# Weights 96 instead of 64 bytes beyond the moving rows, modulo 128, in three stages of a float32r kernel

## The chip, the cores and the metric

The kernel runs on one core of a Trainium2 chip. Its time is the device time of one execution in microseconds; three runs of the kernel before gave 1219.47, 1219.58 and 1220.62 us, median 1219.58.

## The reference

Three layers follow one another; batch 4, sequence 448, width 768 (12 heads of 64).

```python
attn = 1 / (1 + np.exp(-(scale * q @ k.T - np.log(S))))   # sigmoid, per head
x = attn @ v                                              # heads side by side: (4, 448, 768)
xk, xr = (mu * x + (1 - mu) * x_prev for mu in (mu_k, mu_r))
x = 1 / (1 + np.exp(-(xr @ w_r))) * (np.maximum(xk @ w_k, 0) ** 2 @ w_v)
u = x + np.real(np.fft.fft(np.fft.fft(x, axis=1), axis=2))
un = (u - mean) / np.sqrt(var + 1e-06)
out = u + np.maximum(un @ w_ch1, 0) @ w_ch2               # w_ch1: 768 x 3072
```

All is float32. The kernel reaches that precision with float32r matmuls: each operand is split into a high and a low part, and a product is the sum of three matmuls, high by high, high by low and low by high.

## The kernel before, in words

`tile` (L183) makes one output tile of 128 rows by 448 tokens. For each part of the contraction it issues three matmuls: weights high with rows high, weights high with rows low, weights low with rows high. "Weights" are the stationary 128x128 block, "moving rows" the 448 tokens that stream past it. Each matmul has a weight load of its own, which runs while the matmul before it streams.

The stages, in order of time, with their PE tile names:

- attention (`sc`, `av`), with the keys stage (`k<-xkh,wkh` and so on) filled in between;
- receptance (`r<-xrh,wrh`): four batches of 6 x 6 x 3 = 108 matmuls, one after another, with the same weights;
- values (`v<-k,wvh`), with the Fourier stage of each batch in its gaps (`pa`, `qa`, `pq`, `sp`);
- the feed-forward network: first layer (`f<-un,w1h`, and for two of the batches seven products of sums, `f_X`, `f_Y`, `f_Z`, `f_W` `<-B,blk` or `<-T,blk`), second layer (`f<-h,w2h`, `f<-h,v2h`).

The class `Order` (L93) keeps a model of the engines' times and decides by it in which order instructions are issued. It knows sizes, not addresses.

Tiles come from pools that are stacked from the left or the right end of SBUF. A tile's address within its partition follows from what was taken before it in its pool and from the pools below it. `shift` (L256) takes a tile that nobody uses, 16 float32 or 64 bytes, as the first of a pool; all that comes after it in this pool, and in the pools that are stacked on it, lies 64 bytes further. Seven pools have such a tile: `mop` (L341, rows of the keys), `wvp` (L605, weights of the values), `norm` (L662), `wpa` (L964, weights of the second layer), `hp` (L966, hidden rows), `wpb1` (L968) and `wpb2` (L1274, weights of both layers).

Below, the **relation** of a matmul is the address of the weights that are loaded while it streams, less the address of its own moving rows, modulo 256. In the kernel before, by the addresses that the build gives to the tiles:

| stage | weights less rows, mod 128 | of these at relation 192 | at relation 64 |
|---|---|---|---|
| keys | 64 | 557 | 0 |
| receptance | 64 | 215 (batches 1 and 3) | 216 (batches 0 and 2) |
| values | 64 | 1 | 526 |
| network, first layer, `un` | 64 | 843 | 7 |
| network, first layer, `blk` | 64 | 425 | 331 |
| network, second layer, `w2` | 64 | 425 | 437 |
| network, second layer, `v2` | 64 | 425 | 433 |

(Counted are matmuls whose successor on PE is of these stages too; the 128-row score matmuls of the attention have relation 0 to each other and to the key weights that follow them, and the one step from receptance to values has relation 160.)

Of the kernel before, what the change touches and what calls it, by code (L numbers as in the profile page):

```python
# [12 lines left out]
F32 = mybir.dt.float32  # L13
# [231 lines left out]
def build(tc, ap):  # L245
# [5 lines left out]
    def pool(stack, name, bufs=1, side="left", space=None):  # L251
        if space is not None:
            return stack.enter_context(tc.tile_pool(name=name, bufs=bufs, space=space))
        return stack.enter_context(tc.tile_pool(name=name, bufs=bufs, side=side, reuse_waits="tile"))

    def shift(pl, name):  # L256
        pl.tile([128, 16], F32, tag="shift", name=f"shift_{name}", bufs=1)

    def load_split(pl, parts, gap=0.0, raws=1, lane=0, eng=None, vector=False, every=0.0):

# [77 lines left out]
    wra = pool(s_w, "wra", 1, "right")  # L338
    wkp = pool(s_l, "wkp", 1, "left")
    mop = pool(s_l, "mop", 2, "left")  # L340
    shift(mop, "mop")  # L341
    att = pool(s_r, "att", 2, "right")
    ps2 = pool(s_ps, "ps2", 5, space=PSUM)

# [257 lines left out]
    s_l, s_k = ExitStack(), ExitStack()  # L602
    kp = pool(s_k, "kp", 1, "left")
    wvp = pool(s_l, "wvp", 1, "left")
    shift(wvp, "wvp")  # L605
    wvh = wvp.tile([128, NF, D], F32R, name="wvh")
    wvl = wvp.tile([128, NF, D], F32R, name="wvl")

# [50 lines left out]

    s_r, s_f = ExitStack(), ExitStack()  # L660
    np_ = pool(s_r, "norm", 1, "right")
    shift(np_, "norm")  # L662
    wq = pool(s_r, "wq", 1, "right")
    fp = pool(s_f, "four", 1, "right")
    cd = fp.tile([128, 2, CW], F32R, name="cd")
# [295 lines left out]

    s_l = ExitStack()
    wpa = pool(s_l, "wpa", 2, "left")
    shift(wpa, "wpa")  # L964
    hp = pool(s_l, "hp", 2, "left")
    shift(hp, "hp")  # L966
    wpb1 = pool(s_l, "wpb1", 2, "left")
    shift(wpb1, "wpb1")  # L968
    acc, h_t = {}, {}

    def load_acc(b, *keys):
# [299 lines left out]
    s_f.close()  # L1271
    s_b, s_w = ExitStack(), ExitStack()
    wpb2 = pool(s_b, "wpb2", 2, "right")
    shift(wpb2, "wpb2")  # L1274
    tp = pool(s_b, "tp", 1, "right")
    wst = pool(s_w, "wst", 1, "right")
    pools_of = {"w1": (wq, wpb1), "w2": (wpa, wpb2)}
# [78 lines left out]
```

## Time and profile before

| | us |
|---|---|
| median of three runs | 1219.58 |
| the profiled execution | 1218.67 |
| its span, first to last instruction | 1216.9 |
| PE busy | 1203.2 (99%) |
| PE weight loads busy | 1048.5 (86%) |
| DVE busy | 906.9 (75%) |
| ACT busy | 479.3 (39%) |

A matmul's busy time on PE includes the time in its pipeline, so neighbours overlap. What a matmul costs in a dense stream is the distance between two starts, which is read below from stretches with a known number of matmuls. [...]

### The profile page before, as it was taken

The numbers are of one execution on the slowest core, as the hardware profiler recorded it, in microseconds if no ns is written. First come the engines' busy times: TensorE is split into PE (matmuls) and PEld (weight loads), VectorE is DVE, ScalarE is ACT, GpSimd is POOL, SyncE is SP. The second block draws the span as 40 slices with busy tenths as digits, with TensorE's granted clock in tenths as the row PEclk, the third lists the DMA queues.
The fourth block names the chain that finished last, engine by engine and source line by source line (L and its number), as shares of the span: only waits on it lengthen the run. The fifth ranks groups of instructions, "written<-read, shape, count | busy, mean of one in ns | idle before, by whom it ended". The sixth has DMA issues, their size and how long they took to land. (4 is left out here: it accounts for less than half of the span.)

```text
span 1216.9 us, 16416 instructions
## 1 busy us (share of the span) xinstructions
PE 1203.2 (99%) x6142; PEld 1048.5 (86%) x6142; DVE 906.9 (75%) x1425; ACT 479.3 (39%) x864; POOL 135.9 (11%) x97
## 2 busy tenths in 40 slices
PE   8999999999999999999989999999999999999998
PEld 3467767789999999999979999999999999999998
DVE  5676887656852569797999999998566776776654
ACT  5867767657640122142233233333132332322320
POOL 0000000000000000000223232322021111211110
PEclk9999999999999999999999999999999999999999
DMA  6657669666947546387555655655832112122102
GB/s 217 216 175 240 203 244 342 239 242 238 319 164 249 192 167 213 104 315 240 191 186 206 220 186 194 216 202 191 327 134 79 53 59 72 53 67 64 53 1 91
DMA packets 77296, 217.82 MB, mean 179 GB/s; under 512 B 9312, under 2 KB 31776, under 8 KB 76576
## 3 DMA queue, kind: packets, MB, share of 16 engines
q1 hardware_dynamic: 76544, 214.37, 50.9%
q0 software_dynamic: 672, 2.40, 0.6%
q8 instruction: 48, 0.79, 0.3%
q14 instruction: 32, 0.26, 0.1%
HBM read 143.84 MB, written 72.90 MB: 178 GB/s over the span
## 5 line engine op out<-in xcount | busy, mean ns | idle before, releaser
L215 DVE TENSOR_TENSOR acc<-acc,f 128x448 f32<-128x448 f32 x258 | 156.8, 617 | 60.3 <-PE f L180 57.1
L180 PE MATMUL f<-h,w2h 128*128 128x448 f32 x576 | 163.6, 365 | 4.2 <-DVE acc L215 4.2
L180 PE MATMUL f<-un,w1h 128*128 128x448 f32 x576 | 163.7, 364 | 0.0
L180 PE MATMUL f<-h,v2h 128*128 128x448 f32 x576 | 163.1, 364 | 0.0
L180 PEld LDWEIGHTS f<-h,w2h 128*128 128x128 f32 x576 | 107.5, 188 | 13.8 <-DVE acc L215 6.2
L234 ACT ACTIVATE sg<-sc,bias_s 128x448 f32<-128x448 f32 x168 | 95.2, 653 | 61.1 <-PE sc L180 61.1
L180 PEld LDWEIGHTS f<-h,v2h 128*128 128x128 f32 x576 | 108.1, 188 | 7.3
L180 PEld LDWEIGHTS f<-un,w1h 128*128 128x128 f32 x576 | 108.1, 188 | 7.3 <-issue 0.4
L180 PE MATMUL v<-k,wvh 128*128 128x448 f32 x384 | 112.9, 368 | 0.3 <-DMA k<-k_d 0.3
L180 PE MATMUL f<-h,w2l 128*128 128x448 f32 x288 | 104.5, 363 | 0.3 <-POOL w2l L215 0.3
L180 PE MATMUL f<-h,v2l 128*128 128x448 f32 x288 | 104.1, 362 | 0.0
L180 PE MATMUL f<-un,w1l 128*128 128x448 f32 x288 | 103.9, 361 | 0.0
L223 DVE SCALAR_TENSOR_TENSOR w_bits<-w_raw,w_bits 128x768 uint32<-128x768 uint32 x80 | 100.0, 1250 | 1.0
L180 PE MATMUL av<-sg,v 128*64 128x448 f32 (+1 forms) x336 | 81.1, 549 | 0.0
L180 PEld LDWEIGHTS v<-k,wvh 128*128 128x128 f32 x384 | 71.7, 188 | 6.8 <-DMA k<-k_d 1.1
L215 POOL TENSOR_TENSOR v2l<-v,v2h 128x768 fp32r<-128x768 f32 x24 | 47.0, 1975 | 271.7 <-ACT v2h L232 271.7
L215 POOL TENSOR_TENSOR w1l<-w,w1h 128x768 fp32r<-128x768 f32 x20 | 41.9, 2093 | 298.0 <-ACT w1h L232 298.0
L180 PE MATMUL v<-k,wvl 128*128 128x448 f32 x192 | 70.4, 367 | 0.0
L180 PE MATMUL k<-xkh,wkh 128*128 128x448 f32 x192 | 69.9, 364 | 0.0
L180 PE MATMUL k<-xkl,wkh 128*128 128x448 f32 x192 | 69.7, 363 | 0.0
L180 PE MATMUL k<-xkh,wkl 128*128 128x448 f32 x192 | 69.5, 362 | 0.0
L180 PEld LDWEIGHTS av<-sg,v 128*64 128x64 f32 (+1 forms) x336 | 27.8, 143 | 42.5 <-issue 36.0
(175 smaller groups left out, 2354.6 us busy)
## 6 DMA issues: line engine op xcount, KB each, us to landing
w_raw<-in_w SPq DMA_DIRECT2D x40, 768.0 KB, 4.8
w_d<-w SPq DMA_DIRECT2D x40, 384.0 KB, 2.5
k_d<-kp SPq DMA_DIRECT2D x32, 448.0 KB, 2.8
k<-k_d SPq DMA_DIRECT2D x32, 448.0 KB, 5.9
a<-w_d SPq DMA_DIRECT2D x24, 384.0 KB, 3.5
v<-w_d SPq DMA_DIRECT2D x24, 384.0 KB, 3.1
k<-in_k SPq DMA_DIRECT2D x24, 256.0 KB, 5.2
v<-in_v SPq DMA_DIRECT2D x24, 256.0 KB, 3.0
```

The costliest lines, as they stand in the source:

```text
L180: self.nc.tensor.matmul(out, lhs, rhs, start=start, stop=stop, skip_group_check=skip)
L215: eng.tensor_tensor(out, a, c, op=op)
L223: self.nc.vector.scalar_tensor_tensor(out, a, scalar, c, op0=op0, op1=op1)
L234: self.nc.scalar.activation(out, a, fn, **kw)
```

## The change

`shift` gets the number of float32 as an argument. The pools of moving rows get 8 (32 bytes), those of weights 24 (96 bytes); `norm` gets 8, since the tiles of the first layer's weights, `wq`, are stacked on it.

```diff
-    def shift(pl, name):
-        pl.tile([128, 16], F32, tag="shift", name=f"shift_{name}", bufs=1)
+    def shift(pl, name, n):
+        pl.tile([128, n], F32, tag="shift", name=f"shift_{name}", bufs=1)
-    shift(mop, "mop")
+    shift(mop, "mop", 8)
-    shift(wvp, "wvp")
+    shift(wvp, "wvp", 24)
-    shift(np_, "norm")
+    shift(np_, "norm", 8)
-    shift(wpa, "wpa")
+    shift(wpa, "wpa", 24)
-    shift(hp, "hp")
+    shift(hp, "hp", 8)
-    shift(wpb1, "wpb1")
+    shift(wpb1, "wpb1", 24)
-    shift(wpb2, "wpb2")
+    shift(wpb2, "wpb2", 24)
```

No instruction is added, removed or moved: the order on PE, DVE, ACT, POOL and SP is the same row for row. What changes are addresses. By the build's addresses, in keys, values and network the weights now lie 96 bytes beyond the rows modulo 128; modulo 256, all 2676 matmuls of relation 192 get relation 224, and all 1734 of relation 64 get relation 96. Receptance keeps its relations of 64 and 192, the scores theirs of 0. In the Fourier stage rows and weights move together by 32 bytes, and their differences stay.

## Rows read from the trace of the kernel before

**Rows 1.** The page's first part: busy time, share and instructions of each engine.
```profile
PE 1203.2 (99%) x6142; PEld 1048.5 (86%) x6142; DVE 906.9 (75%) x1425; ACT 479.3 (39%) x864; POOL 135.9 (11%) x97
```

**Rows 2.** Busy time of each engine by stage; columns in the first row.
```profile
core 0: us, PE busy (x) PEld busy (x) DVE busy (x) ACT busy (x) POOL busy (x), PEclk, DMA share, GB/s
0.00:330.00 330.00, 324.88 (x1618) 231.22 (x1619) 233.21 (x334) 230.29 (x436) 4.26 (x28) 1.00 0.70 241
...
400.00:590.00 190.00, 189.66 (x1104) 176.93 (x1103) 149.91 (x327) 49.77 (x98) 3.71 (x2) 1.00 0.57 197
590.00:760.00 170.00, 165.53 (x819) 152.73 (x818) 167.45 (x204) 57.74 (x87) 50.19 (x24) 1.00 0.58 203
760.00:1216.90 456.90, 453.12 (x2260) 422.46 (x2258) 323.80 (x510) 124.45 (x218) 74.81 (x38) 1.00 0.32 110
```

**Rows 3.** Timeline of PE and its loads in receptance: start us, us, engine, line, instruction.
```profile
302.90 0.37 PE L180 MATMUL r<-xrh,wrh 128*128 128x448 f32 x1
302.90 0.19 PEld L180 LDWEIGHTS r<-xrl,wrh 128*128 128x128 f32 x1
...
303.11 0.36 PE L180 MATMUL r<-xrl,wrh 128*128 128x448 f32 x1
303.11 0.19 PEld L180 LDWEIGHTS r<-xrh,wrl 128*128 128x128 f32 x1
```

**Rows 4.** Receptance batches 0, 1, 2 and 3, each of 108 matmuls; columns as in rows 2.
```profile
281.05:302.90 21.85, 21.85 (x109) 20.25 (x108) 12.94 (x21) 13.17 (x24) 0.00 (x0) 1.00 0.73 253
302.90:324.51 21.61, 21.61 (x109) 20.25 (x108) 18.60 (x27) 13.14 (x22) 0.00 (x0) 1.00 0.86 286
324.51:346.35 21.84, 21.84 (x110) 20.25 (x108) 16.25 (x24) 13.54 (x23) 0.00 (x0) 1.00 0.89 314
346.35:367.96 21.61, 21.61 (x109) 20.25 (x108) 8.68 (x11) 6.31 (x10) 0.00 (x0) 1.00 0.35 121
```

**Rows 5.** Groups of PE instructions, receptance batch 0: count | busy us, mean ns.
```profile
L180 PE MATMUL r<-xrl,wrh 128*128 128x448 f32 x36 | 13.2, 367 | 0.0
L180 PE MATMUL r<-xrh,wrh 128*128 128x448 f32 x36 | 13.1, 363 | 0.0
L180 PE MATMUL r<-xrh,wrl 128*128 128x448 f32 x36 | 13.0, 361 | 0.0
```

**Rows 6.** The same of receptance batch 3.
```profile
L180 PE MATMUL r<-xrh,wrl 128*128 128x448 f32 x37 | 13.3, 360 | 0.0
L180 PE MATMUL r<-xrl,wrh 128*128 128x448 f32 x36 | 13.1, 363 | 0.0
L180 PE MATMUL r<-xrh,wrh 128*128 128x448 f32 x36 | 13.1, 362 | 0.0
```

**Rows 7.** Timeline, network, first layer: 72 matmuls from one start to the other.
```profile
849.65 0.57 PE L180 MATMUL f<-un,w1h 128*128 128x448 f32 x2
...
864.05 0.57 PE L180 MATMUL f<-h,w2h 128*128 128x448 f32 x2
```

**Rows 8.** Timeline, network, second layer: 72 matmuls from one start to the other.
```profile
1198.19 0.36 PE L180 MATMUL f<-h,v2l 128*128 128x448 f32 x1
...
1212.75 0.37 PE L180 MATMUL f<-h,v2l 128*128 128x448 f32 x1
```

**Rows 9.** Groups by shape, whole span: third product of the scores and of the keys.
```profile
L180 PE MATMUL k<-xkh,wkl 128*128 128x448 f32 x192 | 69.5, 362 | 0.0
...
L180 PE MATMUL sc<-qh,kl 128*128 128x448 f32 x18 | 6.6, 368 | 0.0
```

**Rows 10.** Groups of the first values stretch, with receptance's last matmul.
```profile
L180 PE MATMUL r<-xrh,wrl 128*128 128x448 f32 x1 | 0.4, 370 | 0.0
```

## The prediction, made before the changed kernel ran

> **What bounds the kernel.** I read the busy times first: PE is busy for 99% of the span, and no other engine comes near it over the whole [rows 1]. The stretches by stage say where that could be otherwise [rows 2]. PE lacks 5.1 us of 330 in attention and keys, 0.3 of 190 in values and Fourier, 3.7 of 457 late in the network. Only between 590 and 760 us is another engine as full: DVE is busy for 167.45 of 170 us, PE for 165.53. So outside that stretch whatever PE's matmuls lose or gain goes into the end almost whole. The granted clock is 1.00 in all of these rows.
>
> Since nothing is reordered, the question is only what one matmul costs at another relation of addresses. The timeline shows why a relation could matter [rows 3]: the load of the next weights starts in the same 10 ns as the stream of the current rows, at 302.90 and at 303.11, and lasts 0.19 us of the 0.20 us to the next start. Both read the same memory at the same time.
>
> Receptance measures the relation in the kernel before. Its four batches have the same instructions, shapes, weights and number, 108 matmuls; batches 0 and 2 have relation 64 and batches 1 and 3 relation 192. They take 21.85, 21.61, 21.84 and 21.61 us [rows 4]. Divided by 108 that is 202.3 and 202.2 ns against 200.1 and 200.1. DVE busy (12.9, 18.6, 16.3, 8.7 us), ACT and the share of DMA do not follow this alternation, so traffic of other engines is not the cause. The groups of batches 0 and 3 show it in one matmul's length too: one of the three products has a mean of 367 ns at relation 64, none exceeds 363 at 192 [rows 5, 6]. The network repeats it: 72 matmuls of the first layer, relation 192, take 864.05 - 849.65 = 14.40 us or 200.0 ns each [rows 7]; 72 of the second layer at relation 64 take 14.56 us or 202.2 ns [rows 8].
>
> [...]
>
> **The change part by part.** Nothing is removed or added; shifts of 32 bytes move the matmuls to other relations: 2676 from 192 to 224 and 1734 from 64 to 96. DVE, ACT and DMA also work on tiles that lie 32 bytes elsewhere; I cost that at nothing, since they run beside PE, and only DVE between 590 and 760 us could show it, where it has 2.5 us to spare.
>
> Neither 96 nor 224 stands in the trace in a sustained stretch. The neighbours do.
>
> - For 224: on one side 192 at 200.1 ns, on the other 0 (that is 256). Relation 0 stands in the last product of the 128-row scores, ahead of a key matmul: mean 368 ns against 362 for the keys' third product at relation 192 [rows 9]. Pitch and length go together: in receptance batch 3 the mean length is (360 + 363 + 362) / 3 = 361.7 at a pitch of 200.1, so the length is the pitch plus 161.6, and 368 is a pitch of 206.4.
> - For 96: on one side 64 at 202.2, on the other 160, seen once: receptance's last matmul before the values, 370 ns [rows 10], a pitch of about 208.4.
>
> The rows at 0 and 160 are single places in a sequence, and at relation 64 one product in three reads 367 while the mean of all is 363.7; an average at 0 or 160 may thus lie some 3 ns below what is read. That puts 0 at about 203.4 and 160 at about 205.4. By a straight line, 224 is half the way from 192 to 256: 200.1 + 1.65 = 201.75. Without the correction it would be 203.25. 96 is a third of the way from 64 to 160: 202.2 + 1.05 = 203.25, without the correction 204.3.
>
> I take 1.9 ns more for relation 224, nearer to the corrected value since most matmuls hang on it, and 1.2 ns more for relation 96. The sum: 2676 x 1.9 = 5.1 us, and 1734 x 1.2 = 2.1 us, together 7.2 us. Of the 4410 matmuls about 800 lie in the stretch where DVE is as full as PE [rows 2]; their share of 7.2 us is 1.3, and PE's idle 4.5 us there can hide a part, of which I take 0.5. So the span grows by 6.7 us. The profiled execution took 1218.67 us, 1.8 us outside its span of 1216.9, and that remains; it is 0.9 us below the median of 1219.58. Against the median: 1219.58 + 6.7 = 1226.3 us, say 1226.
>
> Bounds of one matmul, from rows: below, the shortest product group of any stretch is 360 ns [rows 6], a pitch of 198.4; all 4410 there would be 2676 x 1.7 + 1734 x 3.8 = 11.1 us less, 1208.4. Above, all at 206.4 would be 2676 x 6.3 + 1734 x 4.2 = 24.1 us more, 1243.7. A gain can't be excluded: the relation that is best in the trace is known to be better than one other in sustained stretches only.
>
> **The rivals.**
>
> Only the half counts: the pitch depends on whether the weights are ahead by less or more than 128 bytes modulo 256, and anywhere in the lower half it is 202.2, in the upper half 200.1. For it speaks that keys and receptance, whose rows start at 32 bytes modulo 64, and the network, whose rows start at 0, have the same 200.0 to 200.1 at relation 192. Against it, that 0 reads high. Nothing would change: 1219.6 us. [...]
>
> Further ahead is better: the load's reads come clear of the rows sooner, and relation 96 falls to the 200.1 of 192 while 224 stays there. Place: the 1734 matmuls of the values, of half the second layer and of part of the first. Price: 1734 x 2.1 = 3.6 us less, of which some 0.3 is lost between 590 and 760 us, where DVE holds the chain; 1216.3 us. For it: 64 is the worst sustained relation that is known, so any step away from it may help. It decides as soon as relation 224 costs under 3.3 / 2676 = 1.2 ns more. If both fall below 200.1, to the 198.4 of the bound, the time is 1208.
>
> Both are as bad as relation 0: the places that read 368 and 370 are then the rule and 192 is a narrow good spot: 1243.7 us.
>
> **How the numbers follow.** Slower by the straight line, 1226: 0.42. No change, 1219.6: 0.19. Faster at 1216: 0.24, faster towards 1208: 0.07. Slower towards 1244: 0.08. From these, faster by over 0.2% has 0.31, within 0.2% 0.19, slower by over 0.2% 0.50; 0.2%, some 2.4 us, is about what a measurement of this kernel can tell from no change. The range of 8 in 10 leaves out about half of each far case and the edges of the others: 1211 to 1241. The likeliest case alone runs from 1222, where the steps are half as large, to 1231, where no correction is made for single places (2676 x 3.15 + 1734 x 2.1 = 12.1 us).
>
> **What would show it.** Receptance must keep 21.85 and 21.61 us a batch, since its relations stay; if it moves, addresses are not the whole of it. Keys, now all at 224, should show a pitch near 202 before receptance begins. The values, all at 96, should stand near 203.4. Stretches of 72 in the network should alternate between these two, no longer between 200.0 and 202.2. Weight loads should still start with the streams, and their own length stay at 0.19 us. I am wrong if either stretch of 72 comes out at or below its value before, and most of all if the two differ with opposite signs, for then relations would have to be measured one by one.

## The result and the profile after

The changed kernel takes 1231.4 us, median of five runs (1230.32 to 1231.85); the kernel before 1219.58 (1219.44 to 1220.62). The ratio is 1.0093, with a 95% interval of 1.0082 to 1.0105: slower by 11.8 us, where the forecast of 1226 us was 6.4 (and its sum 6.7). The profiled execution took 1231.40 us, 12.7 more than that of before.

The first part of the page, and below it the stages, to be read against [rows 1, 2]; the windows follow the stages, which end later now.

```profile
PE 1217.2 (99%) x6142; PEld 1049.7 (85%) x6142; DVE 907.9 (74%) x1425; ACT 479.1 (39%) x864; POOL 134.9 (11%) x97
```

```profile
0.00:332.00 332.00, 327.10 (x1617) 231.36 (x1618) 233.04 (x334) 230.19 (x436) 4.25 (x28) 1.00 0.70 239
...
402.00:592.00 190.00, 189.31 (x1099) 176.04 (x1098) 149.30 (x326) 49.23 (x96) 3.69 (x2) 1.00 0.57 197
592.00:764.00 172.00, 168.91 (x823) 154.05 (x822) 169.03 (x207) 58.98 (x88) 49.17 (x25) 1.00 0.57 201
764.00:1229.60 465.60, 461.85 (x2260) 422.82 (x2258) 323.76 (x508) 123.39 (x217) 74.85 (x38) 1.00 0.31 108
```

PE is busy for 14.0 us more; no other engine gained more than 1 us, and the loads of weights 1.2. So the matmuls themselves stand further apart. Where, the timeline says. The four batches of receptance, whose relations were kept, in windows as in [rows 4]:

```profile
283.16:305.00 21.84, 21.84 (x109) 20.25 (x108) 13.38 (x22) 13.12 (x24) 0.00 (x0) 1.00 0.75 255
305.00:326.60 21.60, 21.60 (x109) 20.25 (x108) 18.04 (x26) 13.02 (x22) 0.00 (x0) 1.00 0.87 285
326.60:348.45 21.85, 21.85 (x109) 20.25 (x108) 16.27 (x24) 13.49 (x23) 0.00 (x0) 1.00 0.89 315
348.45:370.06 21.61, 21.61 (x109) 20.25 (x108) 8.68 (x11) 6.29 (x10) 0.00 (x0) 1.00 0.35 119
```

They are as before to 0.01 us. Below are the starts at the ends of four dense stretches, from the timeline: 152 keys at relation 224, 162 matmuls of the values at 96, 72 of the first layer at 224, and 72 of the second at 96 [rows 7, 8 are the last two before].

```profile
252.76 0.36 PE L180 MATMUL k<-xkl,wkh 128*128 128x448 f32 x1
...
283.16 0.37 PE L180 MATMUL r<-xrh,wrh 128*128 128x448 f32 x1
...
370.06 0.37 PE L180 MATMUL v<-k,wvh 128*128 128x448 f32 x1
...
402.48 0.44 PE L180 MATMUL v<-k,wvh 128*128 128x448 f32 x1
...
855.62 0.36 PE L180 MATMUL f<-un,w1h 128*128 128x448 f32 x1
...
870.49 0.37 PE L180 MATMUL f<-h,w2h 128*128 128x448 f32 x1
...
1210.62 0.37 PE L180 MATMUL f<-h,v2l 128*128 128x448 f32 x1
...
1225.49 0.36 PE L180 MATMUL f<-h,v2l 128*128 128x448 f32 x1
```

That is 30.40 / 152 = 200.0 ns, 32.42 / 162 = 200.1, 14.87 / 72 = 206.5 and 14.87 / 72 = 206.5. The same relation has two prices: 224 costs 200.0 in these keys and 206.5 in the first layer, 96 costs 200.1 in the values and 206.5 at the end of the second layer. A matmul's mean length shows it too; first the stretch of the first layer at 206.5, then the keys at 200.0:

```profile
L180 PE MATMUL f<-un,w1h 128*128 128x448 f32 x46 | 13.4, 369 | 0.0
L180 PE MATMUL f<-un,w1l 128*128 128x448 f32 x23 | 8.5, 369 | 0.0
```

```profile
L180 PE MATMUL k<-xkh,wkh 128*128 128x448 f32 x46 | 16.7, 362 | 0.0
L180 PE MATMUL k<-xkh,wkl 128*128 128x448 f32 x46 | 16.7, 362 | 0.0
L180 PE MATMUL k<-xkl,wkh 128*128 128x448 f32 x45 | 16.3, 362 | 0.0
```

(These keys are the last of their stage, whose mean is 203.4.) Averaged over all neighbours in the traces that stand under 215 ns apart, relation 224 costs 205.35 ns (2664 of them) where 192 cost 200.19, and relation 96 costs 202.32 (1707) where 64 cost 202.16. That gives 13.7 + 0.3 = 14.0 us. PE's waits give some back: in the second layer (`w2`) what stands above a dense pitch fell from 6.2 to 3.9 us, in the values it rose from 2.7 to 3.4. 14.0 - 2.3 + 0.7 = 12.4 of the 12.7 us.

Two theories went into the experiments. Theory 1: each relation has one price. Theory 2, suggested by these stretches: at some relations a dense stretch of matmuls can settle at either of two pitches, 200.0 or 206.7 ns; it stays at the one it has, and what ran just before selects it.

### The profile page after: what moved, and what is told of

It is laid out like the page before. It is cut to its first block, busy times and chain, and to the rows that moved or that the text cites. A ratio compares the mean times of both kernels' runs of the same rounds, so it can differ in the third digit from the quotient of the medians.

```text
span 1229.6 us, 16416 instructions
## 1 busy us (share of the span) xinstructions
PE 1217.2 (99%) x6142; PEld 1049.7 (85%) x6142; DVE 907.9 (74%) x1425; ACT 479.1 (39%) x864; POOL 134.9 (11%) x97
## 5 line engine op out<-in xcount | busy, mean ns | idle before, releaser
L180 PE MATMUL f<-un,w1h 128*128 128x448 f32 x576 | 166.8, 370 | 0.0
```

The lines of the kernel that those rows point to most:

```text
L180: self.nc.tensor.matmul(out, lhs, rhs, start=start, stop=stop, skip_group_check=skip)
```

## The experiments

**Sixteen relations by themselves.** The stretch as it is written, abridged at `...`; `d` is the relation, `r0` is 0 here, and all addresses are in float32:

```python
r = [r0, r0 + S]
o = (d // 4 + r0) % 64
for t in range(n):
    j = t % KD
    w = [o + 128 * j, o + D + 128 * j]
    ...
    for i, (a, c) in enumerate(((0, 0), (0, 1), (1, 0))):
        nc.tensor.matmul(out, wts[:, w[a] : w[a] + 128], rows[:, r[c] : r[c] + S], ...)
```

> Leaves out the whole computation: it runs only float32r matmuls of the feed-forward network's form (128x128 weights, 448 rows moving, three products each), with no other engine at work, at sixteen relations of weights to moving rows (0 to 240 bytes in steps of 16, modulo 256), 72 matmuls a stretch, once upward, once downward, and then at eight relations each behind a stretch at 192, behind one at 0, and behind a rest of PE. Theory 1, the relation alone sets the price: every visit to a relation shows the same mean pitch, 202.2 ns at 64, 200.1 at 192, about 202.3 at 96 and 205.4 at 224, the means that the two kernels show. Theory 2, two states kept by history: at 96 and 224 a stretch runs either at 200.0 or at 206.7 ns throughout, and which one depends on what ran before it, so that visits to the same relation differ by 6.7 ns.

The pitch into which each stretch settles (mean of its last 30 starts), in ns; where two stand, visits differed:

| relation | 0 | 16 | 32 | 48 | 64 | 80 | 96 | 112 |
|---|---|---|---|---|---|---|---|---|
| ns | 202.7 or 206.7 | 206.7 | 204.4 | 202.2 | 202.2 | 203.3 | 200.0 or 206.7 | 204.0 |

| relation | 128 | 144 | 160 | 176 | 192 | 208 | 224 | 240 |
|---|---|---|---|---|---|---|---|---|
| ns | 204.0 | 204.4 or 202.2 | 205.3 | 203.3 | 200.0 | 204.4 | 200.0 or 206.7 | 203.3 |

The 64 and 192 of this kernel, with no other engine at work (202.2 and 200.0 ns), are those of the full kernel (202.16 and 200.19), so it takes no other engine to make the difference. Four relations have two prices. All values of the table are 200.0 ns plus a simple fraction of 6.67: 1/3 (202.2), 2/5 (202.7), 1/2 (203.3), 3/5 (204.0), 2/3 (204.4), 4/5 (205.3) or the whole (206.7). Busy time in windows of 10 us, columns as in [rows 2], inside relation 224 reached upward (from 208) and downward (from 240), then inside 96 upward (from 80) and downward (from 112):

```profile
221.00:231.00 10.00, 10.00 (x50) 9.09 (x49) 0.00 (x0) 0.00 (x0) 0.00 (x0) 1.00 0.00 0
264.00:274.00 10.00, 10.00 (x52) 9.38 (x51) 0.00 (x0) 0.00 (x0) 0.00 (x0) 1.00 0.01 2
103.00:113.00 10.00, 10.00 (x52) 9.38 (x51) 0.00 (x0) 0.00 (x0) 0.00 (x0) 1.00 0.01 2
381.00:391.00 10.00, 10.00 (x50) 9.06 (x49) 0.00 (x0) 0.00 (x0) 0.00 (x0) 1.00 0.00 0
```

Ten microseconds touch 52 matmuls in one direction and 50 in the other, the same instructions on the same addresses. DVE and ACT are idle and DMA all but idle. Theory 1 fails for 224 and 96; none of the sixteen goes below 200.0.

**Relation 192 everywhere.**

```diff
-    shift(wvp, "wvp")
+    shift(wvp, "wvp", 48)
+    shift(wrp, "wrp", 32)
+    shift(rp, "rp", 32)
+    gap = pool(s_b, "gap", 1, "right")
+    shift(gap, "gap", 32)
     wpb2 = pool(s_b, "wpb2", 2, "right")
```

> The kernel before with relation 192 everywhere in keys, receptance, values and network (128 bytes more in values, and in the pools under the second layer's weights and under receptance's rows). Theory 1 (relation sets the price): 1734 + 216 matmuls fall from 202.2 to 200.1 ns, 4.1 us less, 1215.5 us. Theory 2 (states kept by history, and 192 always in its good state): the same. Rival, that pools or buffers rather than relations make the difference in receptance: no change, 1219.6 us.

1216.19 us (six runs, 1216.08 to 1217.18) against 1219.86; ratio 0.9968, interval 0.9956 to 0.9980. It beats both kernels. 4737 matmuls at relation 192 have a mean pitch of 200.10 ns; by the build's addresses 46 steps between tiles of different pools stand elsewhere, 45 of them at 64. The rival falls: pools and buffers are the same, only their distance changed, and the time fell by 3.7 us; receptance's four batches, all at 192, are among the 4737.

**Relation 224 everywhere, and 96 everywhere** (receptance stays at 192). The shifts of the kernel with 192, with 32 bytes less for rows and 32 more for weights; for 96 the rows' pools get 128 bytes more and the gap goes:

```diff
-    shift(mop, "mop", 16)
+    shift(mop, "mop", 8)      # 40 for relation 96
-    shift(wvp, "wvp", 48)
+    shift(wvp, "wvp", 56)     # 24
-    shift(hp, "hp", 16)
+    shift(hp, "hp", 8)        # 40
...
```

> The kernel with relation 192 everywhere, moved to 224 in keys, values and network (receptance stays at 192). Theory 1 (the relation has one price, the mean 205.35 ns of the changed kernel): 4410 matmuls x 5.3 ns over the 1216.2 us of relation 192, 1239.6 us. Theory 2 (two states, 200.0 and 206.7, kept by history): anything from 1216.2 to 1245.6; since most entries were slow, about 1240 us, and the trace must show stretches wholly at 200.0 and wholly at 206.7, none in between.

1236.92 us (1236.89 to 1237.63), ratio 1.0143, interval 1.0128 to 1.0158; 2.7 us under theory 1's figure and some 3 under theory 2's. Mean pitch 205.69 ns, not below theory 1's 205.35; but between neighbours of these stages PE's waits above a dense pitch fell from 11.2 us (relation 192) to 7.6, which neither expectation had. Of the groups of three successive starts at this relation 3338 take 618 ns or more, 425 take 602 or less, 528 lie between: mostly 206.7, and not none in between as theory 2 had it. That those between are matmuls on the way to a settled pitch is likely from the first experiments and was not counted.

> The same at relation 96 in keys, values and network. Theory 1 (one price, the mean 202.3 ns of the changed kernel): 4410 x 2.3 ns over 1216.2 us, 1226.3 us. Theory 2 (two states): where a stretch is entered from a rest or from 192, 80 or 0 it ran at 200.0 ns, from 112 at 206.7; here nearly all entries come from 96 itself, a wait or another stage, so nearly all fast, 1216 to 1221 us.

1226.38 us, ratio 1.0043, interval 1.0023 to 1.0063. By the number this is theory 1's, but by chance: the mean pitch in the trace is 203.0 ns and not 202.3, and waits took a part back. Theory 2's guess of nearly all at 200.0 was wrong. The trace shows it is not one price: 2354 groups of three take 602 ns or less, 1884 take 618 or more, and only 92 lie between. The runs say the same. Eight of them took 1226.88, 1225.87, 1220.47, 1228.06, 1227.74, 1228.82, 1221.22 and 1221.17 us, a spread of 8.4, while eleven runs of the kernel before beside them lay within 1.5 us. The order of instructions is the same in all eight, so the timing of a run seems to select too; only one of the eight was traced, so that is argued. In the profiled one the first stretch of the values stands at the long pitch and the last of the second layer at the short one, the reverse of the changed kernel at the same relation. These are the starts at the ends of 162 and of 179 matmuls:

```profile
370.57 0.36 PE L180 MATMUL v<-k,wvh 128*128 128x448 f32 x1
...
404.05 0.57 PE L180 MATMUL v<-k,wvh 128*128 128x448 f32 x2
...
1172.57 0.56 PE L180 MATMUL f<-h,v2h 128*128 128x448 f32 x2
...
1208.37 0.36 PE L180 MATMUL f<-h,v2l 128*128 128x448 f32 x1
```

That is 33.48 / 162 = 206.7 ns and 35.80 / 179 = 200.0. Later stretches of the values stand at either pitch (mean of the stage 204.1 ns).

**The network's part alone** (`mop` and `wvp` keep 16).

> The change in the network's five pools alone; keys and values keep 64 bytes. By the stages of the two traces (keys 1.8 us longer and attention 0.5, values 0.3 shorter, network's two layers 11.0 longer between them): about 1229.5 us, most of the 11.8. By the prediction's straight line it would be 4.7 us more than before, 1224.3 us.

1230.76 us against 1219.84, ratio 1.0088, interval 1.0071 to 1.0105: 10.9 us, so keys and values together carry about 1 us of the change, no more than the interval (8.7 to 12.8 us) can hide. The straight line's 4.7 is out.

**Widths, columns and kicks.** A kick is three matmuls at another relation. The stretch of the first experiment with parameters (each three matmuls now also accumulate by themselves):

```diff
-nc.tensor.matmul(out, wts[:, w[a] : w[a] + 128], rows[:, r[c] : r[c] + S], ...)
+nc.tensor.matmul(out, wts[:, w[a] : w[a] + wide], rows[:, r[c] : r[c] + cols], ...)
```

> Leaves out the whole computation: float32r matmuls alone. (a) Weights of 128, 64 and 32 columns at relations 64, 192 and 224, 448 rows. [...] If changing weights has a fixed price, 200 ns stay at 192. [...] (c) 180 matmuls at 224 and at 96, then three matmuls at each other relation with 33 at the base relation between them, then rests of six lengths. Theory 2: the 180 stay in one state; a few of the kicks flip it from 206.7 to 200.0 or back, and it then stays flipped; rests may do so too. Theory 1: no kick or rest changes the mean.

(a) Windows of 5 us with weights of 128 columns (relations 192 and 224), of 64 (224), and of 32 (64, 192 and 224):

```profile
36.00:41.00 5.00, 5.00 (x27) 4.69 (x26) 0.00 (x0) 0.00 (x0) 0.00 (x0) 1.00 0.00 0
52.00:57.00 5.00, 5.00 (x27) 4.69 (x26) 0.00 (x0) 0.00 (x0) 0.00 (x0) 1.00 0.00 0
101.00:106.00 5.00, 5.00 (x26) 3.25 (x25) 0.00 (x0) 0.00 (x0) 0.00 (x0) 1.00 0.00 0
116.00:121.00 5.00, 5.00 (x26) 2.61 (x25) 0.00 (x0) 0.00 (x0) 0.00 (x0) 1.00 0.01 3
133.00:138.00 5.00, 5.00 (x26) 2.60 (x25) 0.00 (x0) 0.00 (x0) 0.00 (x0) 1.00 0.00 0
150.00:155.00 5.00, 5.00 (x26) 2.63 (x25) 0.00 (x0) 0.00 (x0) 0.00 (x0) 1.00 0.00 0
```

The loads get shorter (a mean of 188 ns with 128 columns, 135 with 64 and 108 with 32) and the matmuls no closer: 64 columns settle at 203.3, 201.9 and 206.7 ns for 64, 192 and 224, 32 columns at 206.7 for all three. The idea that the number of weights read while a matmul streams is what it pays for, so that fewer columns would cost less, is refuted, and so is a plain fixed price, since 192 goes from 200.0 to 206.7.

(b) The moving rows get 512, 384 and 256 columns, at eight relations. With 512 the pitch settles at 226.8 ns at relation 0 and at 228.9 to 234.5 at the others, 192 being the lowest of them (228.9); with 384 at 173.3 for 0, 32, 96, 192 and 224, 174.7 for 64, 176.0 for 128 and 176.7 for 160; with 256 at 117.3 to 119.7, 160 aside, whose stretch began with matmuls 213 ns apart at a granted clock of 0.50 and came to 120.0 in its last twelve. So the order of relations is not the same for all column counts: 192 is 2.1 ns above 0 with 512 columns, equal to it with 384, and 2.7 or 6.7 below it with 448.

(c) 180 matmuls at 224 ran at 200.0 throughout, and so did 180 at 96 but for the first few. Three matmuls at relation 0 then left the next 33 at 206.7. Windows in the first stretch, behind that kick, and behind a kick at 96:

```profile
380.00:390.00 10.00, 10.00 (x52) 9.39 (x51) 0.00 (x0) 0.00 (x0) 0.00 (x0) 1.00 0.00 0
392.00:397.00 5.00, 5.00 (x26) 4.55 (x25) 0.00 (x0) 0.00 (x0) 0.00 (x0) 1.00 0.00 0
414.00:419.00 5.00, 5.00 (x27) 4.69 (x26) 0.00 (x0) 0.00 (x0) 0.00 (x0) 1.00 0.00 0
```

A state is kept in a stretch, and what runs in between can change it. Theory 2 holds for 224 and 96. The rests can change it too, and not to one state: 224 settled at 206.7 behind the three shortest and at 200.0 behind the three longest; 96 at 206.7 behind the shortest, at which PE did not stop, and at 200.0 behind the five others.

**The kicks again, four times.**

> Leaves out the whole computation: float32r matmuls alone. Three matmuls at each other relation, then 21 at the base relation, all seven kicks in a row four times over, for base 224 and base 96. If the kick's relation alone selects the state, each kick gives the same state in all four rounds: for 224 fast behind 96 and slow behind 0, 32, 64, 128, 160 and 192; for 96 fast behind 32, 64 and 192 and slow behind 0, 128, 160 and 224. If the state before counts too, some kicks give both. Then eight relations with rows that begin 32 bytes further: if only the relation counts, the same means as with rows at 0 (64: 202.2, 192: 200.0, 32: 204.4, 128: 204.0, 160: 205.3; 0, 96 and 224 one of two). Then six rests before each base: one state each time if a rest resets it, both if not.

For 224: behind a kick at 96 all four stretches settled at 200.0, behind 0, 32, 64, 128, 160 and 192 all 24 at 206.7. For 96: behind 32, 64 and 192 all twelve at 200.0, behind 128, 160 and 224 all twelve at 206.7; behind 0 one at 206.7, reached from a stretch at 200.0, and three at 200.0, reached from stretches at 206.7. The order of the kicks was the same in each round, so nearly every kick met the same state each time. With the run before, the state ahead of a kick differed in three cases: for 224 behind 0 and for 96 behind 32 the outcome was the same, for 96 behind 0 it depended on the state ahead. So what ran just before selects the state, and does so again when repeated; that the kick's relation does it alone is not shown. With rows that begin 32 bytes further the stretches settle at 206.7, 204.4, 202.2, 200.0, 204.0, 205.3, 200.0 and 200.0 ns for relations 0 to 224 in steps of 32, each a value of the table above: the relation counts, and the rows' own address, as far as these 32 bytes go, does not. Behind the rests, six of one length here, 224 settled at 200.0 in all six cases, 96 in five of six; in the first experiment 224 settled at 206.7 behind its rest, so a rest is no sure way to the short pitch.

**The two halves of the change in the kernel.**

```diff
# 192 to 224, 64 stays
+    shift(mop, "mop", 8)
+    shift(np_, "norm", 8)
+    shift(hp, "hp", 8)
+    shift(wpb1, "wpb1", 32)
+    shift(gap, "gap", 16)     # wpb2: none
# 64 to 96, 192 stays
+    shift(wvp, "wvp", 24)
+    shift(wpb2, "wpb2", 32)
+    shift(gap, "gap", 56)
```

> One half of the change: the matmuls of relation 192 go to 224, those of 64 stay. By the means of the two kernels' traces 2676 x 5.2 ns = 13.9 us more, less the 2.3 us of waits in the network that the changed kernel covers: 1231.4 us. By the prediction's straight line 2676 x 1.9: 1224.7 us.

1229.40 us (1228.11 to 1229.97) against 1219.67, ratio 1.0075, interval 1.0059 to 1.0092: 9.7 us, mean pitch 204.87 at 224. Two us under the sum; of these 1.3 are the lower mean pitch (205.35 in the changed kernel, 0.48 ns for each of 2652 matmuls), the rest is within the interval.

> The other half: the matmuls of relation 64 go to 96, those of 192 stay. By the mean of the changed kernel (202.3 against 202.2) no change, 1219.8 us. By theory 2 the mean is whatever share of the stretches falls into the fast state: all fast would be 1734 x 2.2 = 3.8 us less, 1216.0; all slow 1734 x 4.5 = 7.8 us more, 1227.6; and single runs may differ by more than those of the kernel before do. By the prediction's straight line 1734 x 1.2: 1221.9 us.

1220.81 us (ten runs, 1218.93 to 1221.99) against 1219.67, ratio 1.0007, interval 0.9998 to 1.0016. Inconclusive as to its sign, and 1.1 us below the 1221.9 of the straight line, which lies just outside the interval (up to 1221.6). In its trace 898 groups of three stand at the short pitch, 661 at the long one, 100 between. 9.7 + 1.1 = 10.8 of the 11.8 us: the halves add up within their intervals, and relation 224 is most of the change.

## Why the prediction was right, and where it was not

- That PE alone bounds the kernel, and that the relation of weights to rows is what the change moves, held: PE's busy time rose by 14.0 us, its instructions and every other engine stayed, and receptance kept its 21.85 and 21.61 us [rows 4]. With all at 192 the time fell by 3.7 us.
- The term for relation 224 was mis-sized. I took 1.9 ns from a straight line between 192 and 0; it is 5.2 ns on the mean, 13.7 us in place of 5.1. The line was the error, and the correction that went before it was no help: I held the 206.4 read at relation 0 to be 3 ns too high, and relation 0 settles at 206.7 in some visits and at 202.7 in others. There is no slope between neighbours: 192 is 200.0, 208 is 204.4, 224 is 200.0 or 206.7.
- That the time came out inside the stated 1211 to 1241 us, and on the side that had the larger chance, is in part luck. By the pitches of the table, all 4410 matmuls at 200.0 ns would give about 1216 us and all at 206.7 about 1245 (2676 x 6.5 + 1734 x 4.5 = 25.2 us more, if no wait took any of it back). The changed kernel lies between because its stretches fell into both states; the forecast lay between because a line was drawn.
- The term for 96 was 1.2 ns, 2.1 us; measured are 0.2 ns and 0.3 us between the two traces, and 1.1 us, not clear of none, in the kernel with this half alone. Its mean hides the two states.
- The cover in the stretch that DVE fills was taken as 0.5 us. In the second layer PE's waits fell by 2.3 us, more than that, so the sum of terms (14.0 us) reached the end only as 12.7 in the profiled execution.
- The weight loads kept their 0.19 us, and both stretches of 72 rose, as the signs had it. Three signs came out otherwise: the keys ahead of receptance run at 200.0 and not near 202, the values at 200.1 and not 203.4, and both stretches of 72 in the network at 206.5. That one relation could have two prices was in none of the rivals. The first rival, that only the half of 256 bytes counts, falls with the table: 192, 208 and 240 differ (200.0, 204.4 and 203.3 ns). The second, further ahead is better, is true of 96 only where it settles at 200.0. The third, both as bad as relation 0, is what 224 is where it settles at 206.7, and it was given 0.08.
- That the load runs beside the stream [rows 3] was the prediction's reason why a relation could matter. That the load's reads are what a matmul pays for is not shown: addresses move the pitch between 200.0 and 206.7 ns, but loads of a quarter of the columns did not make matmuls cheaper (206.7 ns with 32 columns at 192, 200.0 with 128).

What stays open is the mechanism. The steps are alike (206.7 - 200.0 = 6.7 ns at 96 and at 224), and pitches repeat in a cycle of a few matmuls, 201, 198 and 201 ns at 192, 199, 201 and 207 at 64, and 204, 211, 200, 210 and 195 at 128. What locks there was not tried. Nor is it shown which two addresses count: in each stretch all weights stand alike modulo 256 and all rows too, so the weights loaded beside the rows and the weights that these rows meet have the same relation to them.

## What to carry to other kernels

In a dense stream of float32r matmuls with a load each, read the distance between starts, not the busy share: 99% busy holds 200.0 and 206.7 ns alike. Place weights and rows so that their distance modulo 256 bytes is one that costs little whatever ran before (192 at 448 columns here, 0.3% of the whole kernel), and be wary of a distance that is good in a test by itself: 96 and 224 both reach 200.0 and both fall to 206.7 behind three matmuls at some other relations. A price between two measured points is not to be had by a line when addresses are involved (208, between 192 and 224, cost 204.4 ns here); measure each.

## What the runs showed that was not expected

- The period of the relation is 256 bytes, which the prediction took from receptance and only now is seen elsewhere: 64 costs 202.2 ns and 192 costs 200.0, with 128 bytes between them, while in the kernel before the matmuls whose weights lie 192, 448, 704 and 960 bytes beyond the rows modulo 1024 have means of 200.4, 200.1, 199.7 and 200.5 ns.
- At relations 0, 96, 144 and 224 the same stretch settles at either of two pitches (those of the table), and keeps it for 180 matmuls where that was tried (200.0 ns at 224, and at 96 but for the first few).
- The kernel at relation 96 varies from run to run by 8.4 us in eight runs, where the other kernels, the one before among them, vary by 0.7 to 3.3 us. That its two states are the reason is not shown: the kernel at 224 has two as well, and its four runs lie within 0.7 us.
- Narrower weights made no matmul cheaper: 32 columns cost 206.7 ns at relations where 128 columns cost 200.0 to 202.2.
- The lowest pitches were 226.8 ns with 512 columns, 200.0 with 448, 173.3 with 384 and 117.3 with 256. From 512 to 384 that is 0.42 ns a column. By this price 256 columns are an estimate of 119.8 ns (173.3 - 128 x 0.418), and the lowest that they took is 2.5 less.
